# A shorter hand-over between dependent VectorE operations in a kernel's planner, and another block order in its last step

## The chip, the core and the metric

The kernel runs on one core of one Trainium2 chip. Time is device time in microseconds (us) of one execution; three timed runs of the kernel before took 929.3, 930.08 and 931.87 us, median 930.08. The engines are named as in the profile: PE (TensorE, with PEld for its weight loads), DVE (VectorE), ACT (ScalarE), POOL (GpSimd) and SP (the queue from which the DMAs are issued).

## What is computed

An attention with a compressive memory for 4 batches and 8 heads of 576 tokens with 64 features, then two feed-forward layers over all 2304 tokens (512 features, 2048 hidden):

```
scores = where(causal, -1e9, (q @ k^T) / 8);  a = softmax(scores);  local = a @ v
mem    = (phi(q) @ M_prev) / (phi(q) @ z_prev + 1e-6)         # phi(x) = elu(x) + 1
x      = g * mem + (1 - g) * local                            # g = sigmoid(beta), per head
x      = silu(x @ w_in) @ w_out                               # first layer
out    = mish(x @ w_in2) @ w_out2                             # second layer, mish(h) = h * tanh(softplus(h))
```

All is float32 at the interface; the big products run on float16 pairs (a high part and a rest), three matmuls for each product.

## The kernel before

The program is not written in the order in which it runs. Every operation (a matmul group, an activation, a DMA) is first put on a list with a priority, the regions it reads and writes and an estimated duration (`Plan.add`, L85). `Plan.issue` (L110) then plays the list through: it keeps a clock for each engine, takes the engine that can start next, and gives it, of the operations that are ready by then, the one with the smallest priority number (L165). An operation is ready at the end of each operation it depends on plus a hand-over: `LAT` of the engine that produced it (L67) plus a correction `MORE` for the pair of engines (L68). Only the order that comes out is used; on the chip each engine runs its own list in that order and waits on semaphores. An operation that the plan's clock finds not ready is passed over for a less urgent one that is. SP is one of the engines of the plan, so the order of the DMAs also comes from it.

The stages that matter here:

- Attention runs in steps over pairs of heads. `stage_a` (L564) makes the scores, their row maximum (L613, DVE), the exponentials (ACT) and the split into float16 pairs; `stage_b` (L643) multiplies with v and divides: a chain of small DVE operations (add, reciprocal L683, multiply, multiply). `prep_v` (L530) scales v by a power of two: a reduction (L538), a matmul with ones, two small DVE operations and a reciprocal (L544).
- The weights of the first layer come in 16 units of 1 MB, eight for `w_in` and then eight for `w_out` (`weight_unit`, L790). A unit is loaded (SP), turned from doubles to floats by two ACT operations (L779 and a copy; the copy may be on DVE) and a DVE operation of 1024 columns (L367, `w<-w,ws` or `w<-w`), and eight matmuls add its squares to a Gram matrix. When the eighth unit of a half is in, `part_scale` (L743) takes a scale from the Gram matrix: `diag`, a matmul, a maximum `mx`, and a chain of small DVE operations on `wsc`, `cvec` and `xsc`. Then `weight_split` (L806) makes the float16 pairs of each unit: an ACT copy and a DVE operation, both `w<-w,wsc` with 1024 columns.
- The first layer takes chunks of 256 tokens with eight steps each: `gemm1` (matmuls `xh,w`, 24 a step), the activation, `gemm2` (matmuls `g,w`, 24 a step). `gemm2` cannot start before the first split unit of `w_out`; `gemm1` of the first chunk runs ahead of it.
- The second layer uses seven products for a block product (Strassen's way): `gemm2` (L950) has a step of seven blocks of three matmuls each, named by p = 1 to 7, and `flush2` (L976) combines the seven sums of a chunk: an ACT copy of block 1, then DVE operations on blocks 2 and 6, on 7, on 4 and 5, on 5, and on 3, and two output DMAs. Blocks 2 and 6 share a PSUM bank, 4 and 5 share one, 1 and 7 share one, and the plan has a block write its whole bank. A step's `g` comes in two parts (`hidden2`, L930): first the blocks 1, 2 and 4, later 5, 7, 6 and 3.

While the plan finds PE idle between 18 and 75 us of its own clock it puts in short filler matmuls (L474).

Of the kernel before, what the change touches and what calls it, by code (L numbers as in the profile page):

```python
# [62 lines left out]
class Plan:  # L63
# [1 line left out]


    LAT = {"PE": 197, "ACT": 250, "DVE": 220, "POOL": 130, "SP": 1800}  # L67
    MORE = {("ACT", "POOL"): 20, ("DVE", "POOL"): 20, ("POOL", "PE"): 195, ("PE", "ACT"): 17, ("ACT", "PE"): 150, ("DVE", "PE"): 150, ("SP", "PE"): 150}  # L68

    def __init__(self):  # L70
        self.ops, self.seen, self.shared, self.fill = [], {}, set(), None
# [38 lines left out]
    def issue(self):  # L110
# [13 lines left out]
        def ready(k):  # L124
            for e, _, _, delay in self.ops[k][1]:
                t = 0.0
                for d in self.ops[k][2]:
                    same = on[d] == e
                    t = max(t, end[d] + (0 if same and e == "PE" else self.LAT["SP" if self.ops[d][3] else on[d]] + self.MORE.get((on[d], e), 0)))
                heapq.heappush(wait[e], (t + delay, k))  # L130
# [66 lines left out]
def attn_moe_moe2_kernel(ctx: ExitStack, tc: tile.TileContext, kq, vm, beta, w1, w2, out):  # L197
# [137 lines left out]
    def weight(f, k, part):  # L335
        a = 2048 * (f // 2 + NU // 2 * k) + 1024 * part + 512 * (f % 2)
        return w_first[:, a:a + 512]
# [609 lines left out]
            stt(prio, lo, v, sc[:, 3:4], hi, ALU.mult, ALU.subtract)  # L947
        return g

    def gemm2(l, j, g, yo, prio):  # L950
        if l == 1:
            for p in (2, 1, 4, 6, 7, 5, 3):
                a, b, o = ORDER_A[p], ORDER_B[p], yo[p]
                (gh, gl), (wh, wl) = [g[:, s, a] for s in range(2)], [w_out2[:, j, s, b] for s in range(2)]
                one, end = j == 0 and p in (2, 1, 4, 3), j == NF // 2 - 1 and p in (6, 7, 5, 3)
                mm(prio, [(o, gh, wh, one, False), (o, gh, wl, False, False), (o, gl, wh, False, end)], True)
            return
        for e, m in [(e, m) for e in range(2) for m in range(NC)]:
            gh, gl = g[0][:, e], g[1][:, e]
            f = 2 * j + e  # L960
            wh, wl = weight(f, 1, 0), weight(f, 1, 1)
            first, last = f == 0, f == NF - 1
            s, o = slice(128 * m, 128 * m + 128), yo[m]

            one, end = first and m % 2 == 0, last and m % 2 == 1
            mm(prio, [(o, wh[:, s], gh, one, False), (o, wl[:, s], gh, False, False),
                      (o, wh[:, s], gl, False, end)], True)
# [76 lines left out]
    def weights_of(k, gate=()):  # L1044

        nonlocal n_att
        for u in range(NU // 2 * k, NU // 2 * (k + 1)):
            if u >= U0 and n_att < N0:
                attention(n_att, n_att + 1, s_all)
                n_att += 1  # L1050
            weight_unit(u, w_prio(u), [*gate, *([(f"unit{u - FLIGHT[k]}", 0, 1, 0, 1)] if u >= FLIGHT[k] else [])])
            g, j = divmod(u % (NU // 2), NU // 2 // PARTS)
            if k == 0 and j == NU // 2 // PARTS - 1:
                part_scale(g, w_prio(u))
                for w in range(u - j, u + 1):
                    weight_split(w, w_prio(u))
        if k == 1:
            part_scale(PARTS, w_prio(u))
            for w in range(NU // 2, NU):
                weight_split(w, w_prio(u))  # L1060
# [8 lines left out]
    steps = [(l, c, j) for l, c in chunks for j in range(NF // 2)]  # L1069
    h_att, h_free = [bank[2], bank[3]], [pair(4, 128), pair(6, 128)]  # L1070
    yq = {p: banks[:, 256 * i:256 * i + 256] for i, p in enumerate((2, 6, 4, 5, 1, 7, 3))}
    xs_of, g_of, y_of = {}, {}, {}
# [22 lines left out]
    def first(i):  # L1095

        l, c, j = steps[i]
        prio = MOE + i
        if i == 0:
            inputs(0, 0, prio)  # L1100
        if j == NF // 4 and i + NF // 2 < len(steps):
            inputs(*chunks[i // (NF // 2) + 1], prio)
        if j == 0:
            y_of[l, c] = [bank[m // 2][:, 256 * (m % 2):256 * (m % 2) + TOK] for m in range(NC)] if l == 0 else yq
        if (l, c, j) == (1, 0, 0):
            other(prio, "ACT", 1300, lambda: nc.scalar.preload_act_table_set("mish"), [tables])
        hs = h_att if l == 0 else h_free
        o = hs[i % len(hs)]
        x, sc = xs_of[l, c]
        lead = LEAD if (l, c) == (0, NT // TOK - 1) or (l, c) == (1, 0) and j <= G_AHEAD else max(0, i + 1 + G_AHEAD - len(steps))  # L1110
        gemm1(l, j, x, o, 1e6 + i - 0.5 - lead)
        g_of[i] = (hidden, hidden2)[l](sc, o, prio, j)

    for i, (l, c, j) in enumerate(steps):
        while ahead <= min(i + (1 if l == 0 else G_AHEAD), len(steps) - 1):
            first(ahead)
            ahead += 1
        if i == 0:
            weights_of(1, [(f"step{GATE}", 0, 1, 0, 1)])
            sc = xs_of[0, 0][1]  # L1120
            tt(MOE, sc[:, 2:3], cvec[0][:, 2:3], sc[:, 3:4], ALU.mult)
        gemm2(l, j, g_of.pop(i), y_of[l, c], 1e6 + i)
        if (l, c, j) == (0, NT // TOK - 1, NF // 2 - 2):
            for u in range(NU // 2, LATE):
                weight_pair(u, 1e5 + NU + u)
            for u in range(LATE, NU):
                weight_fetch(u, 1e5 + NU + u)
        if j == NF // 2 - 1:
            (flush, flush2)[l](c, y_of[l, c], xs_of[l, c][1], MOE + i)
# [48 lines left out]
```

## Time and profile before

| | |
|---|---|
| median of three runs | 930.08 us |
| the profiled execution | 929.32 us, of which the span 927.3 us |
| PE busy | 897.8 us (97%) |
| DVE busy | 706.9 us (76%) |
| ACT busy | 594.7 us (64%) |
| POOL busy | 438.5 us (47%) |
| mean granted TensorE clock | 0.997 of full speed |

A window row of the profile gives for a stretch the busy time of each engine with its count of instructions, then the granted clock and the DMA share. A timeline row gives start, duration, engine, source line, operation, what it writes and reads, a count of merged instructions, and in brackets the idle time in front and what ended it. Matmul ends are modelled, and durations of neighbours on one engine overlap a little, so that the distance of two starts says what an operation costs in a dense row.

### The profile page before, as it was taken

The page shows a single profiled execution, that of the slowest core. Times are in us where ns is not written, and L with a number is a line of the kernel's source. Part 1 is how long each engine was busy: PE and PEld are TensorE (multiplying, and loading weights), DVE is VectorE, ACT ScalarE, POOL GpSimd, SP SyncE. Part 2 cuts the span into 40 slices and gives each one's busy share as a digit, 9 for nine tenths or more (in the row PEclk, how much of TensorE's full clock was granted, in tenths as well). Part 3 has the DMA queues.
Part 4 walks back from the last instruction along what each step waited for, and adds up shares of the span by engine and source line. Part 5 has one row for each costly group of instructions (what it writes and reads, how often), then busy time and mean ns, then how long its engine had stood idle before and what let it go on. Part 6 is the DMA issues. An engine that isn't in the chain of part 4 may idle for free.

```text
span 927.3 us, 26260 instructions
## 1 busy us (share of the span) xinstructions
PE 897.8 (97%) x10830; PEld 808.4 (87%) x10830; DVE 706.9 (76%) x1512; ACT 594.7 (64%) x1032; POOL 438.5 (47%) x653
## 2 busy tenths in 40 slices
PE   6889799999999999999999999999999999999997
PEld 5778688888888888888988889999999999999996
DVE  4798977887988688878567465578787887887775
ACT  6799878788687787866465445445455545644553
POOL 3104223645555444564477466363554644635443
PEclk9999999999999999999999999999999999999999
DMA  8799589898999898985434353301010010010010
GB/s 272 260 226 290 161 185 312 204 272 215 240 249 239 241 226 208 231 179 102 115 116 126 136 172 126 104 25 47 19 31 25 25 47 25 24 47 17 10 24 23
DMA packets 148759, 129.77 MB, mean 140 GB/s; under 512 B 105376, under 2 KB 132512, under 8 KB 144544
## 3 DMA queue, kind: packets, MB, share of 16 engines
q1 hardware_dynamic: 148496, 128.10, 52.0%
q8 instruction: 84, 1.38, 0.6%
q14 instruction: 35, 0.29, 0.1%
q10 hardware_dynamic: 144, 0.00, 0.0%
HBM read 77.75 MB, written 25.69 MB: 112 GB/s over the span
## 4 chain that ended last, share of the span: by engine, by line
PE 91%; ACT 4%; DVE 3%; issue 1%; SPq 0%; DMA 0%; DVEq 0%; ACTq 0%
PE banks L427 89%; ACT arena L359 2%; PE banks L435 1%; DVE w L367 1%; ACT w L779 1%; DVE arena L373 1%; ACT w L359 1%; DVE arena L613 0%; PE banks L474 0%; SPq L441 0%; ACT ws L359 0%; DMA arena<-vm 0%; DVE arena L367 0%; DVE ws L367 0%; ACT ga L359 0%
## 5 line engine op out<-in xcount | busy, mean ns | idle before, releaser
L427 PEld LDWEIGHTS <-w 128*128 128x128 f16 (+1 forms) x3584 | 342.0, 98 | 41.1 <-issue 2.1
L427 PE MATMUL banks<-arena 128*128 128x128 f16 (+5 forms) x4728 | 287.2, 221 | 5.8 <-ACT arena L359 4.6
L427 PEld LDWEIGHTS <-arena 128*128 128x128 f16 x4392 | 226.0, 98 | 7.5 <-issue 4.4
L427 PE MATMUL banks<-xh,w 128*128 128x256 f16 x1728 | 206.6, 273 | 0.0
L427 PE MATMUL banks<-g,w 128*128 128x256 f16 x1728 | 205.5, 273 | 0.0
L373 POOL TENSOR_TENSOR arena<-arena 128x4 f32<-128x4 f32 (+3 forms) x147 | 96.8, 663 | 178.6 <-DVE arena L373 78.8
L427 PE MATMUL banks<-w,g 128*128 128x256 f16 x1512 | 178.9, 273 | 0.0
L427 PEld LDWEIGHTS <-g 128*128 128x128 f16 x1512 | 144.4, 98 | 15.2
L373 POOL TENSOR_TENSOR g<-ga,g 128x512 f16<-128x512 f32 x72 | 96.3, 1340 | 69.3 <-ACT g L359 68.9
L359 ACT ACTIVATE arena<-arena 128x256 f32<-128x256 f32 (+7 forms) x169 | 98.9, 606 | 32.7 <-PE banks L427 30.5
L373 POOL TENSOR_TENSOR w<-w 128x128 f32<-128x128 f32 x138 | 78.3, 590 | 87.1 <-ACT w L359 85.5
L367 DVE SCALAR_TENSOR_TENSOR arena<-arena 128x640 f16<-128x640 f32 (+6 forms) x132 | 105.5, 805 | 12.6 <-ACT arena L359 9.6
L373 POOL TENSOR_TENSOR xh<-xh 128x128 f32<-128x128 f32 x138 | 68.2, 516 | 53.7 <-ACT xh L359 51.9
L359 ACT ACTIVATE arena<-banks,arena 128x128 f32<-128x128 f32 (+4 forms) x144 | 74.5, 551 | 21.0 <-DVE arena L613 16.2
L359 ACT ACTIVATE ga<-banks,xsc 128x512 f32<-128x512 f32 x72 | 49.4, 686 | 48.6 <-PE banks L427 46.5
L367 DVE SCALAR_TENSOR_TENSOR g<-w,xsc,g 128x384 f16<-128x384 f32 (+1 forms) x72 | 52.1, 725 | 29.2 <-ACT g L359 29.2
L613 DVE TENSOR_REDUCE arena<-banks 128x2 f32<-128x256 f32 (+3 forms) x80 | 63.6, 802 | 13.8 <-PE banks L427 11.8
L367 DVE SCALAR_TENSOR_TENSOR ga<-ga,banks 128x512 f32<-128x512 f32 x72 | 48.8, 680 | 31.9 <-ACT ga L359 31.6
L359 ACT ACTIVATE w<-banks 128x128 f32<-128x128 f32 x72 | 19.7, 273 | 62.4 <-PE banks L427 62.3
L373 DVE TENSOR_TENSOR arena<-banks,arena 128x8 f32<-128x8 f32 (+1 forms) x96 | 36.3, 378 | 29.4 <-PE banks L427 14.7
L367 DVE SCALAR_TENSOR_TENSOR g<-xh,xsc,g 128x384 f16<-128x384 f32 (+1 forms) x72 | 53.5, 746 | 5.9 <-ACT g L359 4.5
L359 ACT ACTIVATE g<-w,xsc 128x384 f16<-128x384 f32 (+1 forms) x72 | 47.4, 661 | 10.6 <-POOL w L373 10.0
(128 smaller groups left out, 1142.8 us busy)
## 6 DMA issues: line engine op xcount, KB each, us to landing
ws<-w SPq DMA_DIRECT2D x22, 1024.0 KB, 7.0
arena<-kq SPq DMA_DIRECT2D x16, 576.0 KB, 4.8
w<-w SPq DMA_DIRECT2D x8, 1024.0 KB, 5.6
wd<-w SPq DMA_DIRECT2D x16, 512.0 KB, 3.7
arena<-vm SPq DMA_DIRECT2D x16, 325.0 KB, 4.2
yd<-w SPq DMA_DIRECT2D x36, 128.0 KB, 2.7
ws<-wd SPq DMA_DIRECT2D x9, 512.0 KB, 4.3
xs<-yd SPq DMA_DIRECT2D x9, 512.0 KB, 3.7
```

The lines of the kernel that those rows point to most:

```text
L359: return ("ACT", ns, lambda: nc.scalar.activation(out=out, in_=in_, func=func, scale=scale, bias=bias))
L367: return ("DVE", 1.04 * cols(out) + 160 - over[0], lambda: nc.vector.scalar_tensor_tensor(out=out, in0=in0, scalar=s, in1=in1, op0=op0, op ...
L373: return (e, ns, lambda: eng.tensor_tensor(out=out, in0=in0, in1=in1, op=op))
L427: nc.tensor.matmul(out=o, lhsT=l, rhs=r, start=a, stop=z)
L435: plan.add(prio, [("PE", 109, lambda: nc.tensor.transpose(o, x, ident))], [o], [x, ident], edge=(107, 109, (False, False), (False, False)))
L613: other(prio, "DVE", 1.04 * cols(both) + 70, lambda: nc.vector.tensor_reduce(out=m1, in_=both, axis=AX, op=ALU.max, negate=True), [m1], [b ...
L779: plan.add(prio, [("ACT", 0.833 * 1024 + 115, lambda: nc.scalar.activation(out=w, in_=high.bitcast(F32), func=AF.Prelu, scale=2.0**-112, a ...
```

## The change

Two edits. In the planner's table of corrections the pair (DVE, DVE) gets -100: an operation on DVE that needs the result of another one on DVE counts as ready 120 ns after its planned end, where it was 220. And `gemm2` is told when it is the last step of all; for that step it puts its seven blocks on the list in the order 1, 7, 2, 6, 4, 5, 3 where all other steps have 2, 1, 4, 6, 7, 5, 3.

```diff
-    MORE = {("ACT", "POOL"): 20, ("DVE", "POOL"): 20, ...
+    MORE = {("DVE", "DVE"): -100, ("ACT", "POOL"): 20, ("DVE", "POOL"): 20, ...
@@
-    def gemm2(l, j, g, yo, prio):
+    def gemm2(l, j, g, yo, prio, ended=False):
         if l == 1:
-            for p in (2, 1, 4, 6, 7, 5, 3):
+            for p in (1, 7, 2, 6, 4, 5, 3) if ended else (2, 1, 4, 6, 7, 5, 3):
@@
-        gemm2(l, j, g_of.pop(i), y_of[l, c], 1e6 + i)
+        gemm2(l, j, g_of.pop(i), y_of[l, c], 1e6 + i, i == len(steps) - 1)
```

The first edit moves instructions on every engine from the second attention step on; the set of instructions stays the same but for 21 more filler matmuls (431 for 410) and a few operations that may run on either of two engines. Three places:

DVE, the scale of the second half of the weights: `mx` is the maximum, `wsc`, `cvec` and `xsc` the chain of scales, `arena` holds the attention's tiles. Before, beginning at the maximum (12 more rows follow up to the first `w_72<-w_72,wsc_0_89`, the split):

```order
L376 TENSOR_REDUCE mx_84<-banks 128x1
L367 SCALAR_TENSOR_TENSOR arena_95<-arena_95 128x256
L741 RECIPROCAL wsc_0_89<-mx_84 128x1
L367 SCALAR_TENSOR_TENSOR arena_95<-arena_95 128x256
L364 TENSOR_SCALAR wsc_0_89<-wsc_0_89 128x1
L367 SCALAR_TENSOR_TENSOR arena_95<-arena_95 128x512
L364 TENSOR_SCALAR wsc_0_89<-wsc_0_89 128x1
L373 TENSOR_TENSOR arena_95<-banks,arena_95 128x8
L364 TENSOR_SCALAR arena_95<-arena_95 128x2
L613 TENSOR_REDUCE arena_95<-banks 128x2
L373 TENSOR_TENSOR cvec_0_91<-cvec_0_91,wsc_0_89 128x1
L683 RECIPROCAL arena_95<-arena_95 128x8
```

The same place now, from the row behind the maximum to the split:

```order
L538 TENSOR_REDUCE arena_95<-arena_95 128x1
L741 RECIPROCAL wsc_0_89<-mx_84 128x1
L364 TENSOR_SCALAR wsc_0_89<-wsc_0_89 128x1 x2
L373 TENSOR_TENSOR cvec_0_91<-cvec_0_91,wsc_0_89 128x1
L364 TENSOR_SCALAR arena_95<-banks 128x2
L367 SCALAR_TENSOR_TENSOR wsc_0_89<-cvec_0_91 128x2
L364 TENSOR_SCALAR arena_95<-arena_95 128x2
L741 RECIPROCAL cvec_0_91<-cvec_0_91 128x1
L544 RECIPROCAL arena_95<-arena_95 128x1
L364 TENSOR_SCALAR cvec_0_91<-cvec_0_91 128x1
L373 TENSOR_TENSOR xsc_86<-cvec_0_91,xsc_86 128x1
L367 SCALAR_TENSOR_TENSOR w_72<-w_72,wsc_0_89 128x1024 x3
```

From the maximum to the first split there were 23 DVE instructions, nine of them with 256 columns or more; now there are 13, one of them of that size (the reduction L538). In exchange the last unit's own DVE operation of 1024 columns stands as number 162 on DVE where it was 150, and its first ACT operation (L779) as number 142 on ACT where it was 131; the first split is number 184 on DVE where it was 180 and number 154 on ACT where it was 150.

SP, the load of the 16th and last unit of these weights, `w_72<-w`. Before:

```order
L441 DMA ws_77<-w 128x2048
L441 DMA w_72<-w 128x2048
L441 DMA ws_76<-w 128x2048
L441 DMA arena_95<-vm 128x130
L636 DMA_TRANSPOSE arena_95<-arena_95 128x4x128
L441 DMA xd<-arena_95 128x256
L441 DMA arena_95<-kq 128x2x256
```

Now:

```order
L441 DMA ws_77<-w 128x2048
L441 DMA arena_95<-vm 128x260
L636 DMA_TRANSPOSE arena_95<-arena_95 128x4x128
L441 DMA xd<-arena_95 128x256
L441 DMA arena_95<-kq 128x2x256
L441 DMA w_72<-w 128x2048
L441 DMA arena_95<-vm 128x130
```

The load stands behind a transposing DMA, a store of attention output and a load of k and q that it stood ahead of (the seventh transpose, the second such store and the fourth such load of their kinds in both programs).

DVE, the last chunk's `flush2` with the waits of each instruction. Before:

```order
L367 SCALAR_TENSOR_TENSOR ws_76<-banks,xsc_88,w_72 128x512 [waits DMAHW3_49,Activation_49]
L367 SCALAR_TENSOR_TENSOR w_72<-banks,xsc_88,ws_76 128x256 [waits DVE_49,PE_49]
L367 SCALAR_TENSOR_TENSOR ws_76<-banks,xsc_88,w_72 128x512 [waits DMAHW2_49,DVE_49,PE_49]
L367 SCALAR_TENSOR_TENSOR ws_76<-banks,xsc_88,ws_76 128x256
L367 SCALAR_TENSOR_TENSOR ws_76<-banks,xsc_88,ws_76 128x256 [waits DVE_49,PE_49]
```

Now:

```order
L367 SCALAR_TENSOR_TENSOR ws_76<-banks,xsc_88,w_72 128x512 [waits DMAHW3_49,PE_49,Activation_49]
L367 SCALAR_TENSOR_TENSOR w_72<-banks,xsc_88,ws_76 128x256 [waits DVE_49]
L367 SCALAR_TENSOR_TENSOR ws_76<-banks,xsc_88,w_72 128x512 [waits DMAHW2_49,DVE_49,PE_49]
L367 SCALAR_TENSOR_TENSOR ws_76<-banks,xsc_88,ws_76 128x256
L367 SCALAR_TENSOR_TENSOR ws_76<-banks,xsc_88,ws_76 128x256 [waits DVE_49,PE_49]
```

The wait for PE (for block 6) has moved from the second instruction to the first; the instructions stand as they did. PE's own rows read alike there; by the PSUM columns that the built programs' matmuls write, the last step's blocks are issued as 2, 1, 4, 6, 7, 5, 3 before and as 1, 2, 4, 7, 6, 5, 3 now, which is not the order of the new list: the planner passes over block 7 while its part of `g` is not ready by the plan's clock.

## Rows read from the trace of the kernel before

**Rows 1.** Windows: length, busy us of PE, PEld, DVE, ACT, POOL, clock, DMA share, GB/s.

```profile
80.00:100.00 20.00, 17.08 (x197) 14.58 (x195) 18.00 (x44) 17.03 (x36) 8.64 (x8) 1.00 0.91 266
...
850.00:900.00 50.00, 50.00 (x670) 47.28 (x668) 36.94 (x95) 25.38 (x47) 21.41 (x42) 1.00 0.08 23
```

**Rows 2.** Waits of PE, the largest up to 160 us, then all later ones.

```profile
PE banks L427 <- ACT arena L359: 5.3, 2, 4.6
PE banks L427 <- DVE arena L538: 3.9, 1, 3.9
...
PE banks L427 <- ACT arena L359: 0.6, 1, 0.6
PE banks L435 <- DVE mx L376: 0.5, 1, 0.5
```

**Rows 3.** Timeline of PE around the first matmuls of gemm2 (`g,w`).

```profile
96.06 0.49 PE L427 MATMUL banks<-diag,onesf 128*128 128x128 f32 x2 [1.18 <-DVE diag L367]
...
102.26 0.16 PE L427 MATMUL banks<-arena,ones 128*128 128x1 bf16 x1 [3.86 <-DVE arena L538]
...
103.58 1.49 PE L427 MATMUL banks<-g,w 128*128 128x256 f16 x6
```

**Rows 4.** Timeline of DVE: last unit, maximum, end of `wsc`, first split.

```profile
92.19 1.21 DVE L367 SCALAR_TENSOR_TENSOR w<-w 128x1024 uint32<-128x1024 uint32 x1
...
96.60 0.28 DVE L376 TENSOR_REDUCE mx<-banks 128x1 f32<-128x128 f32 x1
...
98.19 0.14 DVE L364 TENSOR_SCALAR wsc<-wsc 128x1 f32<-128x1 f32 x1
...
102.46 2.48 DVE L367 SCALAR_TENSOR_TENSOR w<-w,wsc 128x1024 f16<-128x1024 f32 x2
```

**Rows 5.** Timeline of ACT: the last unit, and the first split.

```profile
89.50 1.16 ACT L779 ACTIVATE w<-w 128x1024 f32<-128x1024 f32 x1
...
101.29 2.18 ACT L359 ACTIVATE w<-w,wsc 128x1024 f16<-128x1024 f32 x2
```

**Rows 6.** Timeline of SP: the 16th unit's load, and the load of k, q.

```profile
82.05 0.33 SPq L441 DMA_DIRECT2D w<-w  x1
...
87.91 0.59 SPq L441 DMA_DIRECT2D arena<-kq  x1
```

**Rows 7.** Groups of ACT from 60 to 103 us: busy us, mean ns, idle before.

```profile
L359 ACT ACTIVATE arena<-arena 128x256 f32<-128x256 f32 x12 | 5.0, 415 | 2.2 <-PE banks L427 2.2
...
L359 ACT ACTIVATE g<-ga 128x512 f16<-128x512 f32 x7 | 4.4, 630 | 0.0
```

**Rows 8.** Windows before the last unit's DVE operation, and around PE's wait.

```profile
60.15:92.19 32.04, 30.49 (x355) 26.67 (x356) 28.98 (x53) 30.86 (x55) 10.30 (x9) 1.00 1.04 266
...
102.00:104.00 2.00, 1.74 (x13) 1.42 (x13) 2.00 (x4) 2.00 (x4) 0.46 (x1) 0.50 0.97 200
104.00:106.00 2.00, 2.00 (x14) 1.15 (x11) 1.68 (x5) 2.00 (x5) 0.20 (x1) 0.65 0.41 140
```

**Rows 9.** DVE: two small dependent operations, then two that are independent.

```profile
35.14 0.20 DVE L683 RECIPROCAL arena<-arena 128x8 f32<-128x8 f32 x1
35.37 0.17 DVE L373 TENSOR_TENSOR arena<-arena 128x8 f32<-128x8 f32 x1
...
68.88 0.69 DVE L373 TENSOR_TENSOR arena<-banks,arena 128x512 f32<-128x512 f32 x1
69.48 1.22 DVE L367 SCALAR_TENSOR_TENSOR w<-w 128x1024 uint32<-128x1024 uint32 x1
```

**Rows 10.** Timeline of all engines at the end.

```profile
911.95 9.33 PE L427 MATMUL banks<-w,g 128*128 128x256 f16 x84
...
920.66 0.47 ACT L359 ACTIVATE w<-banks,xsc 128x256 f32<-128x256 f32 x1 [2.43 <-PE banks L427]
921.17 0.75 DVE L367 SCALAR_TENSOR_TENSOR ws<-banks,xsc,w 128x512 f32<-128x512 f32 x1 [2.15 <-ACT w L359]
922.03 0.48 DVE L367 SCALAR_TENSOR_TENSOR w<-banks,xsc,ws 128x256 f32<-128x256 f32 x1
```

More of the change, by code (lines that the diff above doesn't have):

```diff
@@ L67 @@
     LAT = {"PE": 197, "ACT": 250, "DVE": 220, "POOL": 130, "SP": 1800}
-    MORE = {("ACT", "POOL"): 20, ("DVE", "POOL"): 20, ("POOL", "PE"): 195, ("PE", "ACT"): 17, ("ACT", "PE"): 150, ("DVE", "PE"): 150, ("SP", "PE"): 150}
+    MORE = {("DVE", "DVE"): -100, ("ACT", "POOL"): 20, ("DVE", "POOL"): 20, ("POOL", "PE"): 195, ("PE", "ACT"): 17, ("ACT", "PE"): 150, ("DVE", "PE"): 150, ("SP", "PE"): 150}
     def __init__(self):
```

## The prediction

> **What bounds the kernel now.** I read the windows first. In the first 100 us every engine waits now and then: in the slice from 80 to 100 us PE has work for 17.08 of 20 us while DVE has 18.00 and ACT 17.03. Late in the kernel, from 850 to 900 us, PE is full (50.00 of 50) while DVE has 36.94 and ACT 25.38 [rows 1]. The list of PE's waits says where that begins: the two largest groups of waits up to 160 us come to 9.2 us, and in all the time behind 160 us there are two waits, of 0.6 and 0.5 us [rows 2]. The work of PE behind 160 us does not change in amount. So a change of order can move the end in two places only: in the time at which PE's dense stretch begins, and in the few us behind its last matmul.
>
> The dense stretch begins with the first matmuls of gemm2, `g,w`, at 103.58 us; shortly before them PE stands still for 3.86 us [rows 3]. What they wait for is a chain through three engines: the 16th unit of weights is loaded (issued at 82.05 us [rows 6]), read by ACT at 89.50 us [rows 5], finished by the DVE operation at 92.19 us; its maximum starts at 96.60 us [rows 4], the first split's ACT copy at 101.29 us [rows 5] and its DVE part at 102.46 us [rows 4], 1.1 us before the first `g,w`. The order of PE says that this is the point to watch: at the 25th `g,w` both kernels have issued exactly the same matmuls apart from the 21 fillers. Whatever `g,w` gains, the end gains, as long as no new wait comes up.
>
> **The end (the new block order).** The list order would put block 7 second. The issued order has it fourth, where it was fifth. The ACT copy of block 1 waits for the bank that blocks 1 and 7 share, so it now starts one block earlier. The last 84 matmuls take 9.33 us, 0.111 us each, a block of three 0.33 us [rows 10]. The copy started at 920.66 us, right behind the fifth block, so it goes to 920.33. The first DVE operation followed 0.51 us later, at 921.17 [rows 10]; it now waits also for block 6, the fifth, done by 920.66 at the latest, and the copy is done at 920.84, so it starts at 920.84. The rest of the chain keeps its distances. PE's end stays where it is, and the block that first needs the second part of `g` is the fourth as before, so PE meets no new wait there. Gain: 0.33 us. Bounds: 0 (if the copy is held by something else) and 0.82 us (if the first DVE operation went straight behind the copy of a block 7 issued second: 921.17 less 920.35).
>
> **The hand-over (the head).** First what a hand-over is. Of two small DVE operations in a chain the second starts 0.23 us behind the first; an independent operation starts 0.60 us behind the start of one of 0.69 us [rows 9]. A dependent one starts 0.86 us behind one of 0.75 us [rows 10]. The planner gives the small one 83 ns (L371) and had it followed at 0.30 us, now at 0.20; the wide one 607 ns, followed at 0.83 and now at 0.73 us. So the new number fits the small links (0.23), the old one the wide (0.86). The effect is in the order alone: a chain's next link is picked sooner, and fewer other operations get between.
>
> [...]
>
> Now the chain, step by step, later (+) or earlier (-) than before:
> - The last unit's DVE operation has 12 more operations in front on DVE, and its first ACT operation 11 more in front on ACT. On ACT these are seven of at most 256 columns, taken at 0.415 us, and four of 512, at 0.63 us [rows 7]: 2.9 + 2.5 = 5.4 us, less some 0.1 us each by which neighbours overlap in such a dense row, 4.3 us. DVE's twelve come to less (three have a handful of columns, and one of 1024 goes away), so ACT decides. Its 30.86 busy of 32.04 us in the stretch before [rows 8] leave at most 1.18 us of waits in which that could disappear. +3.1 to +4.3 us.
> - From the last unit's DVE operation to the maximum it took 4.41 us [rows 4]. The rows in between leave 3.3 us now: the operation itself 1.2, eight Gram matmuls 0.6, `diag` and its matmul 0.8, the rest DVE work in front. -1.1 us.
> - From the maximum to the first split's ACT copy it took 4.69 us [rows 4, 5], of which 1.73 up to the end of `wsc` at 98.33 us. Now the reduction L538 and three small links stand in between: 0.28 for the maximum, about 0.33 for L538 and 3 x 0.22, 1.27 us. -3.4 us.
> - From that copy to the DVE part 1.17 us, unchanged.
>
> Sum: -1.4 to -0.2 us; I take -0.8. The outer bounds come from what the trace does not show. Upwards: the load of the 16th unit stands behind a transpose, a store and a load that were issued up to 87.91 us before [rows 6]. If these come no earlier than they did, the load goes out at 88.5 instead of 82.05 us; with the same 7.45 us up to ACT, that is 95.95 instead of 89.50, +6.45 in place of +4.3, and the sum is +1.9. In the new order the stores' ACT copies stand some 4 us of ACT work earlier, which is why I do not take this. Downwards: if DVE as well as ACT lose their waits fully and links cost 0.12 less each, -2.2.
>
> The 21 fillers stand in waits before 75 us and count nothing; were all of them in the way, 0.03 us each would make 0.6 us, and that before a wait of 3.86 us. In the second layer DVE and ACT have a quarter to a half of their time free [rows 1]; reordering there is covered by PE.
>
> Total: -0.33 - 0.8 = -1.1 us on an execution of 929.32 us (span 927.3 and 2.0 around it): 928.2. The median of the runs is 0.76 us above this execution; on it the same sum gives 929.0. I say 928.6, between the two.
>
> **Rivals.**
> 1. The two halves of the head cancel: the chain is shorter by what the unit comes later, `g,w` start within 0.4 us of 103.58. Only the end's 0.33 us is left: 929.0 to 929.7. For it: DVE has done nearly the same work at the first split (number 184 for 180). Against: the chain's saving is counted link by link.
> 2. The clock. Behind PE's wait of 3.86 us the granted clock was 0.50 for 2 us and 0.65 for 2 more, the lower level of 1.2 GHz for most of that time [rows 3, 8]; at the higher level the same work would have taken 1.0 + 0.7 = 1.7 us less. If the new order breaks this wait into pieces (the ones matmul now stands right behind the short chain) the clock may stay up: -1.1 - 1.7 and up to 0.6 of shorter waits, 925.8. For it: a wait of 1.18 us at 96.06 did not lower the clock. Against: PE has as little work as before between the Gram matmuls and `g,w`. The Trainium skill (TensorE: Matmul & The Clock Gate, "HAM oscillation") says that idle gaps between bursts put the array back to the lower clock; the trace agrees with its 0.50.
> 3. Slower: the 16th load. SP issues in order, so if the transpose or the store in front of it waits for attention work as it did, the load goes out at 88.5 us, everything behind it moves: +1.9 - 0.33 is 930.9, and with PE idle 2 us longer the lower clock could cost one more us, 931.9. It decides from a load issued later than about 87 us. For it: the order of SP. Against: attention stands earlier in the new order on ACT and DVE.
> 4. The change doesn't do what its list says: the last step's blocks are not issued in the listed order. That is in the forecast. Were they, the end would gain 0.82 us: 928.1.
>
> **How the numbers follow.** Chances: forecast (927.4 to 929.5) 0.45, rival 1 0.22, rival 2 0.15, rival 3 0.15, rival 4 0.03. A measurement of this kernel can tell about 0.3%, 2.8 us, from no change. Faster by more than that, below 927.3, needs rival 2 or the low end of the forecast: 0.21. Slower, above 932.9, needs rival 3 with more than I count: 0.11. The rest, 0.68, is within. The range 926.0 to 931.6 leaves out the far ends of rivals 2 and 3.
>
> **What would show it.** Right: the first `g,w` at 102.5 to 103.3 us; from the maximum to the first split's ACT copy 1.2 to 1.6 us instead of 4.69; the last unit's L779 at 92.5 to 94 us; block 1's copy 0.33 us closer to PE's start of the last step, and from PE's last matmul to the end 0.33 us less. Wrong: the 16th load issued behind 87 us (rival 3), clock 1.00 throughout (rival 2), a wait of PE above 1 us behind 110 us that was not there, or the copy of block 1 still right behind the fifth block.

## The result and the profile after

The changed kernel took 936.05 us (median of four runs, 935.41 to 936.74); the kernel before took 929.71 beside it. The ratio is 1.0060 with an interval of 1.0048 to 1.0072: 6.3 us slower. The forecast was 928.6 us, 1.1 us faster, with a range up to 931.6. It was wrong in sign and outside its range.

The profiled execution has a span of 933.6 us (927.3 before) and a mean granted clock of 0.983 (0.997). Beginning with the end, the place that went as forecast. This is the timeline of PE, ACT and DVE behind the last step's matmuls in the kernel after (start, us, engine, line, operation; idle time and its end in brackets), to be read beside [rows 10]:

```profile
918.62 9.33 PE L427 MATMUL banks<-w,g 128*128 128x256 f16 x84
...
927.01 0.47 ACT L359 ACTIVATE w<-banks,xsc 128x256 f32<-128x256 f32 x1 [2.11 <-PE banks L427]
...
927.51 0.75 DVE L367 SCALAR_TENSOR_TENSOR ws<-banks,xsc,w 128x512 f32<-128x512 f32 x1 [1.83 <-ACT w L359]
928.30 0.48 DVE L367 SCALAR_TENSOR_TENSOR w<-banks,xsc,ws 128x256 f32<-128x256 f32 x1
```

The copy of block 1 starts 8.39 us behind the last 84 matmuls' start where it was 8.71, the first DVE operation 8.89 where it was 9.22. From that start to the end of the span it is 15.0 us, 15.4 before. But the 84 matmuls start 6.67 us later. So the loss lies ahead of them.

The two windows that answer to [rows 1], of the kernel after (length, busy us of PE, PEld, DVE, ACT, POOL, clock, DMA share, GB/s), look much as they did for PE, which says that averages over 20 or 50 us don't show where 6 us went; in the first of them ACT is 1.8 us busier:

```profile
80.00:100.00 20.00, 17.27 (x194) 14.58 (x192) 17.24 (x35) 18.84 (x34) 8.72 (x9) 1.00 1.08 335
...
850.00:900.00 50.00, 50.00 (x665) 47.12 (x664) 37.79 (x95) 24.31 (x45) 21.81 (x38) 1.00 0.07 20
```

Next PE around the first `g,w` (timeline of PE, kernel after; [rows 3] are the rows of before):

```profile
97.08 0.83 PE L427 MATMUL banks<-arena 128*128 128x65 f16 x14
100.66 1.03 PE L427 MATMUL banks<-w 128*128 128x128 bf16 x8 [2.76 <-DVE w L367]
102.08 0.80 PE L427 MATMUL banks<-diag,onesf 128*128 128x128 f32 x2 [0.38 <-DVE diag L367]
103.58 0.16 PE L427 MATMUL banks<-arena,ones 128*128 128x1 bf16 x1 [0.71 <-DVE arena L538]
103.61 0.67 PE L435 MATMUL banks<-ident,arena 128*128 128x128 f32 x2
105.82 0.39 PE L427 MATMUL banks<-g,w 128*128 128x256 f16 x1 [1.54 <-ACT w L359]
107.14 0.61 PE L427 MATMUL banks<-g,w 128*128 128x256 f16 x2 [0.93 <-DVE w L367]
107.54 2.71 PE L427 MATMUL banks<-arena 128*128 128x65 f16 x16
```

One wait of 3.86 us has become five waits of 6.3 us together. The first `g,w` starts 2.24 us later, and it is not yet the dense stretch: the second waits another 0.93 us. The clock is low all the while: the 16 matmuls of the last row took 2.71 us here, and 1.50 us in a kernel of this study (fillers in bank 0, below) that ran the same rows at the full clock. The windows of the kernel after, which answer to [rows 8] (columns as above):

```profile
102.00:104.00 2.00, 1.21 (x5) 0.82 (x5) 1.90 (x8) 0.12 (x1) 0.77 (x1) 0.50 0.76 166
104.00:106.00 2.00, 0.46 (x3) 0.11 (x1) 1.10 (x9) 1.65 (x3) 0.20 (x1) 0.50 0.66 189
106.00:108.00 2.00, 1.07 (x10) 0.74 (x9) 2.00 (x2) 1.99 (x3) 0.00 (x0) 0.50 0.03 11
108.00:110.00 2.00, 2.00 (x12) 1.30 (x10) 1.98 (x3) 2.00 (x4) 0.00 (x0) 0.50 0.00 0
```

The lower level (1.2 GHz) holds from 100.6 to 110.9 us, 10.2 us; before, it held from 102.0 to 105.4, 3.4 us.

Why was the first split late? The chain upstream, in three timelines of the kernel after. DVE (13th unit's last operation, 16th unit's, maximum, first split's DVE part; [rows 4]):

```profile
84.42 1.23 DVE L367 SCALAR_TENSOR_TENSOR w<-w 128x1024 uint32<-128x1024 uint32 x1
...
99.39 1.22 DVE L367 SCALAR_TENSOR_TENSOR w<-w 128x1024 uint32<-128x1024 uint32 x1
...
102.91 0.29 DVE L376 TENSOR_REDUCE mx<-banks 128x1 f32<-128x128 f32 x1
...
105.80 3.79 DVE L367 SCALAR_TENSOR_TENSOR w<-w,wsc 128x1024 f16<-128x1024 f32 x3 [0.85 <-ACT w L359]
```

ACT (13th unit, 16th unit with the row in front of it, first split; [rows 5]):

```profile
81.10 1.14 ACT L779 ACTIVATE w<-w 128x1024 f32<-128x1024 f32 x1
...
95.11 0.83 ACT L359 ACTIVATE arena<-banks,arena 128x256 f32<-128x256 f32 x2
95.82 1.15 ACT L779 ACTIVATE w<-w 128x1024 f32<-128x1024 f32 x1
...
104.63 2.17 ACT L359 ACTIVATE w<-w,wsc 128x1024 f16<-128x1024 f32 x2
```

SP (13th unit's load, then the load of k and q and the 16th unit's load; [rows 6]):

```profile
74.37 0.42 SPq L441 DMA_DIRECT2D w<-w  x1
...
85.24 0.59 SPq L441 DMA_DIRECT2D arena<-kq  x1
85.92 0.54 SPq L441 DMA_DIRECT2D w<-w  x1
```

and, for comparison, the 13th unit's load in the kernel before:

```profile
66.85 0.33 SPq L441 DMA_DIRECT2D w<-w  x1
```

The 16th unit is loaded into the place that the 13th has just left, so its load can go out only when DVE has finished the 13th. In the kernel before, that DVE operation stood at 80.34 us, SP waited for it, and the load went out at 82.05. Now the operation stands at 84.42 and ends at 85.65, and the load goes out at 85.92; by then SP has no wait for DVE left, but it has just issued the load of k and q that the new order puts in front (85.24 to 85.83). The freed place and SP's order hold the load to within 0.2 us of the same time, and the trace does not separate them. The 13th unit was late already: its load went out at 74.37 us, before at 66.85, behind other entries of SP's list, of which one had waited 3.2 us for DVE. What began that I did not trace.

The 16th unit's data landed at 92.0 us, 6.1 us behind the issue (before: 87.0, 4.9 us behind it). ACT did not wait for them: the timeline has no idle time in front of the operation at 95.82, which comes 3.8 us behind the landing (before 2.5). What stands in front of it on ACT is work. Up to that operation ACT was busy for 77.45 of 95.82 us, before for 72.64 of 89.50 (windows of the two kernels): 4.8 us more work, and 1.5 us more idle time, taken over the whole head. In the planner the operation goes to ACT as soon as its data count as landed; a later load in the plan therefore puts more work in front of it, and the chip runs that list, whether the data are there earlier or not. So ACT read the unit 6.32 us later than before, DVE finished it at 99.39 (7.2 later), and the shorter chain up to the first split gave 3.9 us of it back.

To see what each part costs PE I made an account. For every form of matmul I took the median distance to the next one behind 130 us in these two traces. What a stretch takes beyond the sum of these distances is called lost. Stretches end where equally much work is left (820, 800 and 21 us of it), so that kernels can be compared; idle time of PE and its work at the low clock are given for the second.

| us lost | up to 84 us | 84 to about 112-116 us | of it idle | worked at low clock | from there to the last step |
|---|---|---|---|---|---|
| before | 24.2 | 7.6 | 5.2 | 3.1 | 9.9 |
| after | 24.4 | 11.8 | 7.0 | 6.7 | 11.8 |

The second stretch loses 4.25 us more: 1.8 are idle time, and 3.5 us more work at half the clock cost another 1.8 if each us of it loses half; the remaining 0.7 I did not resolve. The rest of the kernel loses 1.9 us more. At equal work left the kernel after is 0.5 us later at 84 us; so are three kernels below that have the 410 fillers of before (end alone, hand-over behind the head only, late load), so this is no cost of the 21 additional fillers that a trace shows, but lies within what executions differ by. With the 0.4 us gained at the end the sum is 6.3 us.

The 1.9 us are spread. The windows of before and after from 216 to 318 us show the largest part; the first row is of the kernel before:

```profile
216.00:318.00 102.00, 102.00 (x1195) 88.47 (x1194) 85.70 (x164) 78.72 (x132) 53.26 (x70) 1.00 0.95 227
```

and this one of the kernel after:

```profile
216.00:318.00 102.00, 100.64 (x1180) 86.47 (x1178) 86.55 (x163) 81.11 (x136) 51.62 (x68) 1.00 1.00 235
```

PE was full there and now is not. The waits of PE behind 160 us in the kernel after (total us, times, longest) were two rows in [rows 2] and are seven now:

```profile
PE banks L427 <- ACT arena L359: 0.5, 1, 0.5
PE banks L427 <- DVE arena L373: 0.4, 1, 0.4
PE banks L435 <- DVE arena L373: 0.4, 1, 0.4
PE banks L435 <- DVE arena L364: 0.3, 1, 0.3
PE banks L427 <- DVE xsc L364: 0.3, 1, 0.3
PE banks L427 <- DVE ws L367: 0.3, 1, 0.3
PE banks L427 <- DVE arena L538: 0.2, 1, 0.2
```

### The profile page after: what moved, and what is told of

Read it like the earlier page. It is cut to its first block, busy times and chain, and to the rows that moved or that the text cites. A ratio compares the mean times of both kernels' runs of the same rounds, so it can differ in the third digit from the quotient of the medians.

```text
span 933.6 us, 26288 instructions
## 1 busy us (share of the span) xinstructions
PE 902.6 (97%) x10851; PEld 809.1 (87%) x10851; DVE 718.8 (77%) x1515; ACT 599.5 (64%) x1035; POOL 447.5 (48%) x647
## 4 chain that ended last, share of the span: by engine, by line
PE 88%; DVE 6%; ACT 3%; DMA 1%; issue 1%; POOL 0%; SPq 0%; DVEq 0%; ACTq 0%
PE banks L427 87%; DVE arena L367 1%; ACT arena L359 1%; PE banks L435 1%; DVE arena L373 1%; ACT w L359 1%; DVE w L367 1%; DMA ws<-w 1%; ACT w L779 1%; DVE arena L613 0%; DVE ws L367 0%; DMA arena<-vm 0%; PE banks L474 0%; DVE xh L367 0%; POOL arena L373 0%
## 5 line engine op out<-in xcount | busy, mean ns | idle before, releaser
L427 PE MATMUL banks<-g,w 128*128 128x256 f16 x1728 | 208.1, 273 | 2.5 <-ACT w L359 1.5
L373 POOL TENSOR_TENSOR arena<-arena 128x64 f32<-128x64 f32 (+3 forms) x147 | 100.7, 689 | 183.2 <-DVE arena L373 102.7
L373 POOL TENSOR_TENSOR g<-ga,g 128x512 f16<-128x512 f32 x72 | 98.5, 1368 | 77.1 <-ACT g L359 73.0
L373 POOL TENSOR_TENSOR xh<-xh 128x128 f32<-128x128 f32 x141 | 77.2, 568 | 84.0 <-ACT xh L359 82.1
L359 ACT ACTIVATE arena<-arena 128x256 f32<-128x256 f32 (+6 forms) x172 | 99.9, 605 | 16.3 <-PE banks L427 13.9
L367 DVE SCALAR_TENSOR_TENSOR g<-w,xsc,g 128x384 f16<-128x384 f32 (+1 forms) x72 | 55.9, 779 | 17.9 <-ACT g L359 17.5
L367 DVE SCALAR_TENSOR_TENSOR ga<-ga,banks 128x512 f32<-128x512 f32 x72 | 49.0, 680 | 25.6 <-ACT ga L359 25.5
L359 ACT ACTIVATE g<-ga 128x512 f16<-128x512 f32 x70 | 44.1, 630 | 26.1 <-DVE ga L367 22.2
L359 ACT ACTIVATE g<-xh,xsc 128x384 f16<-128x384 f32 (+1 forms) x72 | 47.2, 661 | 11.0 <-POOL xh L373 8.9
```

The source lines that it names most:

```text
L359: return ("ACT", ns, lambda: nc.scalar.activation(out=out, in_=in_, func=func, scale=scale, bias=bias))
L367: return ("DVE", 1.04 * cols(out) + 160 - over[0], lambda: nc.vector.scalar_tensor_tensor(out=out, in0=in0, scalar=s, in1=in1, op0=op0, op ...
L373: return (e, ns, lambda: eng.tensor_tensor(out=out, in0=in0, in1=in1, op=op))
L427: nc.tensor.matmul(out=o, lhsT=l, rhs=r, start=a, stop=z)
```

## The experiments

My theory after the result: the order of the first 110 us decides; the late 16th unit and the longer low clock behind it are most of the loss ("head theory"). Rivals: the shorter hand-over spoils the dense stretch; the time follows the hand-over's size. All kernels have the new block order. Ratios are to the kernel before on the same chip, with 95% intervals; medians of different kernels were mostly taken on different chips.

### One part of the change at a time

Only the end:

```diff
-    MORE = {("DVE", "DVE"): -100, ("ACT", "POOL"): 20, ...
+    MORE = {("ACT", "POOL"): 20, ...
```

> The changed kernel without the shorter hand-over: only the last step's block order is changed. Head theory (the lost time comes from the order of the first 110 us, which only the hand-over moves): the order up to the last 84 matmuls is that of before, y leaves about 0.3 to 0.4 us earlier, 929.0 to 929.7 us. Rival (the last step is part of the loss): above 930.5 us.

Measured 929.94 us, 0.9996 (0.9987 to 1.0006). In its trace PE's last 84 matmuls start at 912.67 and block 1's copy at 921.05, 8.38 us behind. The median is 0.2 us above the range that I expected. By the trace the new block order is worth its 0.3 to 0.4 us, too little for the timing to show, and it has no part in the loss.

The shorter hand-over only in the head, and only behind it (`end[d]` is the plan's time at which the producer ends):

```diff
-                    ... + self.MORE.get((on[d], e), 0)))
+                    ... + (self.MORE.get((on[d], e), 0) if (on[d], e) != ("DVE", "DVE") or end[d] < 104e3 else 0)))
```

> The shorter hand-over is used only up to 104 us of the list schedule's own clock, which ends just behind the first g,w; from there on the old 220 ns; block order as changed. Head theory: 16th unit's load again at about 86 us, first g,w at about 105.8, low clock for about 10 us, so most of the loss is there: 933.5 to 936 us. Rival (the shorter hand-over spoils the order of the dense stretch, and the head's lateness is made good there): 929 to 931.5 us.

The other way round, with `end[d] > 101e3`:

> The shorter hand-over is used only from 101 us of the list schedule's own clock on; the head is ordered as before; block order as changed. Head theory: load of the 16th unit at 82, first g,w at 103.6, 929 to 931.5 us (up to 1.9 us of waits between 140 and 290 us may belong to this part). Rival (dense stretch): 933 us or more.

Head only: 933.45 us, 1.0030 (1.0018 to 1.0042); first split at 105.16, first `g,w` at 106.36. Behind it only: 930.40 us, 0.9999 (0.9990 to 1.0009). The account has 11.8 us lost in the second stretch and 9.1 behind it for the head only, 7.6 and 9.9 for the other. So the head loses the same 4.2 us as the changed kernel, and the shorter hand-over used behind it does no harm by itself: the rival falls. But behind this head it makes 2.7 us of difference (11.8 against 9.1): about half of the total loss is not in the head, and neither part alone shows it.

### The late 16th unit alone

The hand-over of before; the plan may issue the 16th unit's load only 4.7 us after it could:

```diff
-            prio, [("SP", 475, lambda: nc.sync.dma_start(out=out, in_=in_))],
+            prio, [("SP", 475, lambda: nc.sync.dma_start(out=out, in_=in_), late)],
@@
-        dma(prio, r, W[l][u].bitcast(U32)..., reads=[*gate])
+        dma(prio, r, W[l][u].bitcast(U32)..., reads=[*gate], late=4700 if (l, u) == (0, 15) else 0)
```

> The hand-over of before (220 ns), the new block order, and one thing more: the list schedule may issue the 16th unit's load only 4.7 us after it could, about as late as the changed kernel has it. If the late 16th unit is the cause of the head's loss: load near 86 us instead of 82, first split near 105 instead of 101.8, the low clock lasts about 10 us instead of 3.4, and 932.5 to 936 us. If the head's loss comes from the other moves that the shorter hand-over makes there: 929.5 to 931 us.

Measured 933.12 us, 1.0028 (1.0018 to 1.0039), as much as the head only. The timelines of SP, ACT and PE in this kernel, the load, the first split and the first `g,w`:

```profile
87.15 0.56 SPq L441 DMA_DIRECT2D w<-w  x1
```

```profile
104.51 2.19 ACT L359 ACTIVATE w<-w,wsc 128x1024 f16<-128x1024 f32 x2 [0.58 <-DVE wsc L367]
```

```profile
106.88 0.27 PE L427 MATMUL banks<-g,w 128*128 128x256 f16 x1
108.65 5.33 PE L427 MATMUL banks<-g,w 128*128 128x256 f16 x32 [1.50 <-DVE w L367]
```

The low clock lasted 6.8 us in two pieces, not 10. In the account the second stretch loses 11.0 us, 3.2 more than with the end alone (7.8). So a late load in the plan, with the hand-over of before, is enough for the head's loss. It is not one instruction moved, though: from there on the planner deals the lists of all engines anew, as in the changed kernel. Here too the data were in place (landed at 93.4 us) when ACT came to the unit at 95.49, without idle time in front. So the loss goes with the order that a late load brings; that the chip waits for the load itself the traces do not show.

### The unit early again, with the shorter hand-over

```diff
-    MOE, W_PRIO, ATT_B = MOE_B, (-2e5, 20.0), -2.1e5
+    MOE, W_PRIO, ATT_B = MOE_B, (-2e5, 18.0), -2.1e5
```

> The changed kernel with the weight units of the second half at priority 18 plus their number instead of 20 plus it: the hand-over stays at the shorter value, but the 13th unit's last VectorE operation and so the 16th unit's load are ordered earlier again (the list schedule puts the load 5.4 us and the first split 4.8 us ahead of where the changed kernel has them). Head theory: first split on ScalarE near 100 us instead of 104.63, 927 to 930.5 us. Rival (the shorter hand-over itself spoils the order): 934 us or more.

Measured 931.39 us, 1.0002 (0.9991 to 1.0012), 4.7 us less than the changed kernel. Load at 81.0 us, first split at 99.92, earlier than in the kernel before; yet no faster than that one, against my expectation. The windows of this kernel point to the clock:

```profile
100.00:102.00 2.00, 2.00 (x20) 1.35 (x18) 1.06 (x3) 2.00 (x3) 0.00 (x0) 0.50 0.85 214
...
106.00:108.00 2.00, 2.00 (x13) 1.42 (x11) 2.00 (x2) 1.84 (x4) 0.00 (x0) 0.50 0.04 12
```

PE is full of work and at half its clock. From 98.9 to 109.1 us it did 9.2 us of work at that level, by the account 4.6 lost.

### The clock

Filler matmuls into the idle stretches; the other engines' orders stay word for word. First into bank 7, where the kernel's own fillers write; in the changed kernel 172 of them, 137 in the one with priority 18 (with 85e3 and 96e3), and 133 with the end alone (85e3 and 94.5e3):

```diff
-                if FILL_FROM < t < FILL_TO:
+                if FILL_FROM < t < FILL_TO or 88e3 < t < 99e3:
```

> The changed kernel with 172 more filler matmuls (28 ns each, they write scratch columns that nothing reads) in the idle stretches of TensorE between 97 and 107 us; nothing else moves on any engine. If the low clock is a part of the loss (TensorE did 6.7 us of its work at the low clock between 84 and 116 us, 3.1 us in the kernel before, so 3.3 against 1.6 us lost to it): the granted clock stays at 1.00, first g,w unmoved, 932.5 to 934.5 us. If the low clock costs nothing beside the waits: 935.5 to 937 us.

> The kernel with the second half's weight units at priority 18 plus their number, with 137 more filler matmuls in the idle stretches of TensorE between about 94 and 104 us. There 9.2 us of work ran at the low clock, 4.6 us lost. If the clock is what holds this kernel, whose first split came 4.7 us earlier than in the changed one, at only 931.4 us: the clock stays at 1.00 and the time is 926.5 to 929 us. If not: 930.5 to 932 us.

> The hand-over of before, the new block order, and 133 more filler matmuls (28 ns each, scratch columns) in the idle stretches of TensorE between 94 and 102.3 us, 98 of them in the one long wait; no other engine's order moves. If the low clock behind that wait is a loss of its own (3.1 to 3.4 us of work at half the clock, so 1.6 us), and the fillers fit into the wait: granted clock 1.00 throughout, first g,w within 0.5 us of where it was, 928.2 to 929.4 us, below both kernels. If the fillers come in the way of the chain to the first split, or the clock falls all the same: 930 to 931.5 us.

Measured: 937.58 us, 1.0078 (1.0063 to 1.0093); 929.74 us, 0.9989 (0.9979 to 0.9998); 932.19 us, 1.0019 (1.0010 to 1.0028). None came as expected; the second gained 1.65 us on its kernel without fillers, the other two lost. The timeline of PE in the third shows what went wrong:

```profile
101.77 4.36 PE L474 MATMUL banks<-mask,ident 128*128 128x60 bf16 x97 [3.08 <-DVE cvec L364]
105.97 0.17 PE L427 MATMUL banks<-arena,ones 128*128 128x1 bf16 x1
```

The fillers waited 3.08 us themselves and then ran, most of them at the low clock (it held from 102.1 to 105.5 us), in front of what PE had to do. In the program the first of them waits for DVE, whose attention operations read other columns of bank 7. The Trainium skill (PSUM — Partial Sum Buffer, "PSUM bank collisions raise a hardware error") tells of a scheduler that lets two engines wait for one another on the same bank and partitions, whatever the columns; the wait here is of that kind. So the same fillers into bank 0, which nothing uses between the scale of the first half and the first `g,w`:

```diff
-        plan.fill = lambda: nc.tensor.matmul(out=bank[7][:, 452:512], ...
+        plan.fill = lambda b: nc.tensor.matmul(out=bank[b][:, 452:512] if b else bank[0][:, 0:60], ...
```

> The changed kernel with 172 fillers in bank 0 between 97 and 107 us. If the low clock behind the late split is a loss of its own, as the accounts of the trace have it (6.7 us of work at half the clock, 3.3 us): the clock stays at 1.00, first split and first g,w stay where they are, and 932.5 to 934.5 us. If it is not: 935.5 to 937 us.

> The kernel with the hand-over of before, the new block order and 133 more fillers, which now write columns of bank 0, idle at that time, instead of bank 7, which VectorE reads during the wait. If the fillers of bank 7 only failed because they waited for VectorE: they run inside the long wait from 98.4 us on, the granted clock stays at 1.00, first g,w is not later, and 927.8 to 929.2 us, some 1.6 us less than without them. If the low clock is no loss: 929.5 to 930.5 us.

> The kernel with priority 18 plus the number and 137 fillers in bank 0 instead of bank 7. With fillers of bank 7 it took 929.74 us, and TensorE waited 0.8 and 0.4 us at the fillers themselves. If these waits held the chain up: 928 to 929.3 us, clock 1.00. If not: 929.5 to 930.2 us.

The changed kernel with them (172): 934.59 us, 1.0040 (1.0027 to 1.0054), against 936.05. With the end alone: 929.23 us, 0.9987 (0.9978 to 0.9996), against 929.94. With priority 18: 929.28 us, 0.9983 (0.9974 to 0.9993), against 931.39. The timeline of PE in the kernel with the end alone, where fillers now fill 2.8 us of the long wait and the clock stays at 1.00:

```profile
98.96 2.83 PE L474 MATMUL banks<-mask,ident 128*128 128x60 bf16 x97
102.98 0.16 PE L427 MATMUL banks<-arena,ones 128*128 128x1 bf16 x1 [1.19 <-DVE arena L538]
```

All three lie at the slow edge of what I expected or a little beyond it. The windows from 84 to 116 us, first of the changed kernel as it was, then with fillers in bank 0; the clock is the third figure from the end:

```profile
84.00:116.00 32.00, 25.05 (x242) 19.91 (x240) 28.11 (x64) 27.53 (x48) 8.48 (x10) 0.84 0.79 231
```

```profile
84.00:116.00 32.00, 28.83 (x435) 24.98 (x433) 28.19 (x63) 28.95 (x50) 10.09 (x11) 1.00 0.97 240
```

So the low clock looks like a loss of its own, but a smaller one than half of the work done at it: by the medians 1.5 us in the changed kernel (the account has up to 3.3), 0.7 in the order of before, 2.1 where most work ran at it. By the ratios, each to the kernel before on its own chip, these are 1.9, 0.8 and 1.8 us, and in each pair the two intervals overlap; that all three go the same way carries this reading more than any one of them. The waits for the late split stay: the changed kernel with its clock held is still 1.0040. The other two are faster than the kernel before, by 1.3 and 1.2 us.

Is the loss behind the head due to the shorter hand-over used there? The kernel with priority 18 and bank-7 fillers, with the condition `end[d] < 104e3`:

> The kernel with the second half's weight units at priority 18 plus their number and the fillers (929.74 us), with the shorter hand-over used only up to 104 us of the list schedule's own clock, and 220 ns behind it. If the shorter hand-over behind the first g,w makes a worse order of the dense stretch given this head, as the head-only kernel against the changed one suggests (2.7 us less lost behind 116 us): 927 to 929 us. If the stretch is only dealt anew, to either side: 928.5 to 932 us.

930.21 us, 0.9999 (0.9990 to 1.0007), against 929.74: no gain. With this head the old hand-over is no better behind it.

### Other sizes of the hand-over

Only the number in the table differs (-160, -40, -120, -20, +50).

> The changed kernel with -160 for -100, so a hand-over of 60 ns instead of 120 ns. Head theory (only where the order happens to put the 13th unit's last operation, the 16th unit's load and the first split decides, not the size of the hand-over): here the list schedule puts the load 5.6 us and the first split 6.2 us ahead of where the changed kernel has them, so the first split on ScalarE stands near 98.4 us, and the time is 925 to 930.5 us (with the low clock lasting 10 us, the upper part of that). Rival (the shorter the hand-over, the worse the order): 937 us or more.

> The changed kernel with -40 for -100, so a hand-over of 180 ns, nearer to the 220 ns of before. Head theory: here the list schedule puts the first split as late as in the changed kernel and the first g,w 1.8 us later still, so the loss is there with two fifths of the change: 933 to 938 us, first split near 104.7, first g,w at 105.5 or later. Rival (loss in step with the size of the change): 931 to 932.5 us.

> The changed kernel with -120 for -100: one more value of the hand-over. If every value deals the whole order anew, with no trend in the value (so far 929.9 at 0, 934.1 at -40, 936.05 at -100, 932.95 at -160): anywhere from 929 to 937 us, and not between its neighbours as a matter of course. If the time follows the value: 934 to 936 us.

> The changed kernel with -20 for -100. If every value deals the order anew: 929 to 937 us, and by the list schedule's first split, which is 0.4 us earlier than at 0, rather 929 to 932 us. If the time follows the value: 930.5 to 932.5 us.

> The changed kernel with +50 for -100, so a longer hand-over than before (270 ns). If every value deals the order anew, and the order of before is only the best of those met: 929.5 to 937 us, most likely above 930.5. If it is the shortening that costs: 928.5 to 930 us.

| DVE to DVE | us | ratio (interval) | first split | lost up to 84 | to 112-116 | behind |
|---|---|---|---|---|---|---|
| 270 ns | 932.21 | 1.0016 (1.0005 to 1.0026) | 101.51 | 23.3 | 10.6 | 10.4 |
| 220 ns (end alone) | 929.94 | 0.9996 (0.9987 to 1.0006) | 101.82 | 24.9 | 7.8 | 9.9 |
| 200 ns | 933.59 | 1.0022 (1.0006 to 1.0037) | 102.14 | 23.6 | 8.4 | 15.0 |
| 180 ns | 934.11 | 1.0039 (1.0024 to 1.0054) | 102.78 | 24.4 | 9.6 | 12.4 |
| 120 ns (the change) | 936.05 | 1.0060 (1.0048 to 1.0072) | 104.63 | 24.4 | 11.8 | 11.8 |
| 100 ns | 932.38 | 1.0018 (1.0007 to 1.0028) | 103.25 | 25.9 | 7.9 | 10.6 |
| 60 ns | 932.95 | 1.0027 (1.0017 to 1.0038) | 100.88 | 25.5 | 7.4 | 12.7 |

The time does not follow the size: 120 ns is the worst, 100 ns much better, 200 ns worse than 100. All six other values are slower than 220 ns, the longer one too, each with its loss in another place. Three of my expectations fell here. The 180 ns kernel's time came as expected, but not by the way that I had given: its split should have stood near 104.7 us and stands at 102.78. The 60 ns kernel should have gained by its early split; the plan's clock had it 2.9 us ahead of the kernel before, the chip 0.4 us, and it loses behind the head. The 200 ns kernel has the split almost where it was and loses 5 us behind it. So the head theory holds for the change at hand and is no rule for the kernel: the first split is one place of several.

## Why the prediction was wrong

- The end: right. 0.32 us at the copy for 0.33 forecast, 0.4 at the end of the span. The dependent pair of wide DVE operations, read as 0.86 us before, is 0.79 apart here, where the second one waits for DVE alone.
- "On ACT these are seven of at most 256 columns ... +3.1 to +4.3 us": this step failed. The last unit's ACT operation came 6.32 us later. That ACT decides was right: it had no idle time in front of the operation, and the data had landed 3.8 us before. The size was wrong on both sides. The eleven more operations were 4.8 us more work instead of 4.3, and ACT's idle time up to there, which I let shrink by up to 1.18 us, grew by 1.5. I had priced the added work by average rows and let ACT's idle time go one way only, while the whole list had been dealt anew.
- Rival 3, the late load: it named the right unit and SP's order as what holds it. The load went out at 85.92 instead of 82.05, behind the load of k and q as this rival had it, though the freed place would have held it about as long; its bound of 87 us was not reached. Its time for ACT's operation, 95.95, lies next to the measured 95.82, but that is luck: it counted 7.45 us from the load to ACT, and it was 9.90, with the data waiting for ACT and not the other way round.
- The step from the last unit's ACT operation to its DVE operation was not in the sum at all: 3.57 us, 2.69 before, another +0.9.
- From that operation to the maximum: -1.1 forecast, -0.9 measured (3.52 for 4.41). From the maximum to the first split: -3.4 forecast, -3.0 measured (1.72 for 4.69). From the copy to the DVE part: unchanged, 1.17. These held. The shorter chain is there and gives 3.9 us; it only starts 7.2 us later. With the two misses the sum is +3.3 instead of -0.8. The first `g,w` itself came 2.24 us later: it now starts with the split's DVE part, where it stood 1.1 us behind it before.
- "Whatever `g,w` gains, the end gains, as long as no new wait comes up": new waits came up. 0.93 us in front of the second `g,w`, and the low clock, which I had taken as unchanged, lasted three times as long. The sign that I had given for a wrong prediction, a wait above 1 us behind 110 us, did not come; the waits stood just ahead of that mark.
- The clock, rival 2: I thought that pieces of a wait might keep it up. The Trainium skill's rule (TensorE: Matmul & The Clock Gate, "HAM oscillation") that bursts between gaps fall back to the lower clock was the better guide, and the trace agrees: with the wait in pieces PE was busy for 6.78 of the 13 us from 98 to 111 (9.14 before; windows of the two kernels), and the clock stayed low 10.2 us instead of 3.4.
- "Reordering there is covered by PE" behind the head: failed by 1.9 us, mostly between 216 and 318 us, in the first layer, where DVE is busy 86 of 102 us and covers little. Shown is that it depends on head and hand-over together; which operation starts it stays open.
- "The 21 fillers ... count nothing": nothing that the runs show speaks against it. The 0.5 us by which the kernel after is late at 84 us are there without these fillers too.
- The plan knew part of it. By its own clock the changed order has the 16th load 4.7 us and the first split 3.4 us later (chip: 3.9 and 3.3). I read positions and not these times. They are no safe guide either, as the 60 ns kernel shows.

The range was too narrow for this reason: it was made from one chain, while the edit deals the whole order anew. Six other values of the same number spread from 932.2 to 936.05 us.

## What to carry to other kernels

A constant in a scheduler's cost table is no local edit: it deals the order of every engine anew, and the effect has the spread of such deals, here 2.3 to 6.1 us to the worse by the medians for each of six other values, whatever the constant means on the chip. When a chain gets shorter, look at what its first link waits for: at the landing of its data, and at the end of the work in front of it on its engine, and take the later of the two. Here the work in front was the later one by 3.8 us, and its amount came from where the plan expected the data. Fillers that are to hold the clock up want a place that no other engine reads: here those in a bank that DVE reads waited 3.08 us with the rest, and those in an unused bank did not.

## What the runs showed of the hardware

- How long the low clock lasted did not go by the longest wait: 3.4 us behind a single wait of 3.86 us; 10.2 us where five waits between 0.38 and 2.76 us came one after another; 10.2 us (98.9 to 109.1) in the kernel with priority 18, whose largest wait was 1.8 us; 6.8 us in two pieces in the one with the late load, with six waits between 0.33 and 2.16 us. Nor does it go by the number of waits, and what decides it these runs do not show.
- In one stretch a low clock cost nothing that these runs show. From 10 to 30 us the profiled execution of the kernel after ran at a granted clock of 0.57 and the head-only kernel, with the same order there, at 1.00 (windows of the one and of the other); up to 84 us they lost 24.4 and 24.9 us. Of the eleven runs with priority 18 and fillers in bank 0, six with a mean clock of 0.987 to 0.989 have a median of 928.8 us, and five with 0.996 to 0.999 one of 929.35; in which stretch the clock of the six was low no trace shows.

```profile
10.00:30.00 20.00, 17.29 (x126) 14.62 (x126) 10.66 (x27) 10.99 (x21) 2.02 (x4) 0.57 0.94 337
```

```profile
10.00:30.00 20.00, 17.26 (x118) 14.47 (x119) 9.84 (x25) 11.19 (x22) 2.02 (x4) 1.00 0.90 328
```

PE gets through as many matmuls in the 20 us with the low clock as without (126 and 118), and its waits in this stretch come to 4.0 us in both, most of them for ACT: its own clock does not set its pace there.
